# Edge rows of M as 32x32 TensorE tiles, four chunks at once, and M made by column halves

## The chip, the cores and the metric

The kernel runs on one core of one Trainium2 chip. The metric is device time in microseconds (us) of one execution. Besides the timed runs there is one profiled execution; its trace gives every duration below.

## What is computed

The reference is a sum of two blocks over the same 2048 x 640 activations `x`, in bf16:

```python
def reference(A_x, A_wqkv, A_wo, B_x, B_w_r, B_w_gate, B_w_up, B_w_down):
    def _A_ref(x, wqkv, wo):                      # linear attention, H = 32 heads of Dh = 20
        ...
        phi = lambda t: jnp.where(t > 0, t + 1, jnp.exp(t)) + 1e-6
        pq, pk = phi(q), phi(k)
        kv = jnp.einsum("bhsd,bhse->bhde", pk, v)
        z = jnp.einsum("bhsd->bhd", pk)
        num = jnp.einsum("bhqd,bhde->bhqe", pq, kv)
        den = jnp.einsum("bhqd,bhd->bhq", pq, z)[..., None] + 1e-6
        o = num / den
        return (lambda x, *d: x.transpose(*d))(o, 0, 2, 1, 3).reshape(B, S, D) @ wo
    def _B_ref(x, w_r, w_gate, w_up, w_down):     # 8 rows, chosen by x @ w_r, pass a gated MLP
        ...
        return x + upd.reshape(B, S, D)
    x = A_x
    xn = _layernorm(x, axis=-1)
    return x + _A_ref(xn, A_wqkv, A_wo) + _B_ref(xn, B_w_r, B_w_gate, B_w_up, B_w_down)
```

Since `num` is linear in `kv`, and `wo` follows it, the kernel makes one matrix M = blockdiag(kv) @ wo, of 640 x 640, and the output is the normalized phi(q) times M.

## The kernel before

The work is one program with its order written out by hand: each engine runs its instructions in the order of the code, and DMAs wait in the queue of the engine that issues them (SyncE, called SP, for nearly all).

**First part, up to about 52 us of the span.** For each of 16 token tiles of 128 rows: layer norm on VectorE and ScalarE, a transpose of xn (`tr_dma`, by DMA), the k projection on TensorE (`K`, L241), phi on ScalarE and VectorE, and the accumulation of G = xn^T phi(k) in PSUM (`G`, L281 and L286). `loads(t)`, called at the end of tile t, issues loads for later: at t = 13 wq, wo1 (the first 128 of each 160 rows of wo), wo2 (the last 32 of each 160 rows; chunk g lies on partitions 32g to 32g+31) and the gate weights.

**Middle part, to about 83 us.** phi(q) is made in 20 pieces: `q_pe(tb, m, bank)` (L489) is five matmuls of 512 columns, whose result ScalarE passes through Exp and Relu (L495, L496); `q_fin` (L544) joins the two on VectorE. Between these pieces stand kv, M, the denominators and the routed rows:

- `kv_pe` multiplies wv with G. Heads are 20 wide, and a chunk g of 160 columns holds eight of them; its block diagonal is cut into four row blocks of 32 (L633), which fill the 128 rows of `kv1`, and an edge of 32 rows (L640), which goes to `kv2`. `kv_ev` masks both on VectorE: four instructions for kv1 (L649) and four for the edges (L654), which put chunk g's edge on partitions 32g to 32g+31 and in columns 160g+120 to 160g+159 of `kv2`. Everything else of kv2 is zero.
- M has five row chunks of 128 rows (m = 0 to 4). In each, rows 32g to 32g+31 come from kv chunk g, by a slice of kv's columns with step 5 that starts at m (`by5`). `m_tiled(m, b)` (L659) makes them from kv1 as four 128x32 tiles side by side, for both column halves, into banks b and b+1. `m_full(m, b, eng)` (L665) adds the edges of all four kv chunks with one 128x128 matmul per half and evicts the chunk (L672 on VectorE, L670 on ScalarE) to `Mb`.
- `route1` and `route2` find the eight rows; `route2` ends with eight copies on GpSimd (L614) that gather xn's columns into `xsT`, each behind a register load. `gu_pe` (L683) is the gate and up projection, `y_pe` (L705) the down projection.
- `den` (L553) makes the denominators, `norm` (L579) multiplies phi(q) by their inverse.

The order around the change is: `kv_pe`, `kv_ev`, q_pe(0,4), q_fin(0,3), q_pe(1,0), q_fin(0,4), `route2`, q_pe(1,1), then m_tiled(0), m_tiled(1), m_full(0), m_full(1); three q pieces later the same for m = 2 and 3; four q pieces later m_tiled(4), and behind `den` and `gu_pe` m_full(4).

**Last part.** For each token tile ten matmuls with Mb (`out_mm`, L721), an addition on VectorE (L735) and a store.

Of the kernel before, what the change touches and what calls it, by code (L numbers as in the profile page):

```python
# [7 lines left out]
P = 128  # L8
S = 2048
D = 640  # L10
# [5 lines left out]
NG = 4  # L16
GC = D // NG
# [5 lines left out]
FQ = F // 4  # L23
# [6 lines left out]
BF16 = mybir.dt.bfloat16  # L30
F32 = mybir.dt.float32
I32 = mybir.dt.int32
I16 = mybir.dt.int16
AF = mybir.ActivationFunctionType
ALU = mybir.AluOpType
# [3 lines left out]
def kernel(  # L39
# [13 lines left out]
    pe, dve, act, pool, sp = nc.tensor, nc.vector, nc.scalar, nc.gpsimd, nc.sync  # L53
# [11 lines left out]
    PS = psp.tile([P, 8, 512], F32, name="PS")  # L65

    def st(shape, dt, name, tag=None):
        return sb.tile(shape, dt, name=name, tag=tag or name)
# [5 lines left out]
    wk = st([P, KC * (D + 1)], BF16, "wk", "wkM")  # L74
    wq = st([P, KC, D], BF16, "wq")
    wo1 = st([P, NG, D], BF16, "wo1")
    wo2 = st([P, D], BF16, "wo2")
    wv = st([P, KC, D], BF16, "wv")
    Gs = st([P, KC, D], BF16, "Gs")
    wg = st([P, KC, F], BF16, "wg")  # L80
# [5 lines left out]
    bm2 = st([P, GC], BF16, "bm2")  # L86
# [10 lines left out]
    HW = 320  # L97
# [4 lines left out]
    def ld(eng, dst, src):  # L102
        eng.dma_start(dst, src)
# [20 lines left out]
    def warm(n, w=512):  # L124
# [6 lines left out]
        out=ident[:], in_=ident[:], compare_op=ALU.not_equal, fill=1.0,  # L131
# [9 lines left out]
    kv1 = st([P, NG, GC], BF16, "kv1")  # L141
    kv2 = st([P, NG, GC], BF16, "kv2")
# [195 lines left out]
    wo_v = A_wo.rearrange("(g r) d -> r g d", r=GC)  # L338
    wg_v = B_w_gate.rearrange("(kc p) n -> p kc n", p=P)
    wu_v = B_w_up.rearrange("(kc p) n -> p kc n", p=P)  # L340

    def loads(t):
        if t < 5:
            ld(sp, XX[:, 6 + 2 * t : 8 + 2 * t, 1, :], x_v[:, 6 + 2 * t : 8 + 2 * t, :])
        if 7 <= t < 7 + KC:
            ld(sp, wv[:, t - 7, :], wqkv_v[:, t - 7, 2 * D : 3 * D])
        if t == 6:
            late["wvb"] = st([P, D], BF16, "wvb", "junk")
            ld(sp, late["wvb"][:], A_wqkv[ZD : ZD + 1, 2 * D : 3 * D].to_broadcast([P, D]))
        if t == 13:  # L350
            ld(sp, wq[:], wqkv_v[:, :, 0:D])
            ld(sp, wo1[:], wo_v[0:P, :, :])
            for g in range(NG):
                ld(sp, wo2[32 * g : 32 * g + 32, :], A_wo[GC * g + P : GC * (g + 1), :])
            for k in range(KC):
                ld(sp, wg[:, k, :], wg_v[:, k, :])


    ld(sp, XX[:, 4:6, 1, :], x_v[:, 4:6, :])
    loads(0)  # L360
    for t in range(1, 5):
        loads(t)
# [78 lines left out]
    for t in range(4, T):  # L441
# [36 lines left out]
        if t > 4:  # L478
            loads(t)


    def by5(ap):
        return ap.rearrange("p (q m) -> p m q", m=KC)
# [3 lines left out]
    def q_pe(tb, m, bank):  # L487
        for kc in range(KC):
            pe.matmul(  # L489
                PS[:, bank, :], lhsT=by5(wq[:, kc, :])[:, m, :], rhs=xnT[:, kc, tb * TBLK : (tb + 1) * TBLK],  # L490
                start=(kc == 0), stop=(kc == KC - 1),
            )
        e = tmp.tile([P, D], BF16, tag="ek", name="qe", bufs=3)[:, 0:TBLK]
        r = tmp.tile([P, D], BF16, tag="rk", name="qr", bufs=3)[:, 0:TBLK]
        act.activation(e, PS[:, bank, :], AF.Exp)  # L495
        act.activation(r, PS[:, bank, :], AF.Relu)  # L496
        qst[(tb, m)] = (e, r)
# [41 lines left out]
    Mb = st([P, KC, D + 1], BF16, "Mb", "wkM")  # L539
    rd_d = drp.tile([2, H, 8 * P], BF16, name="rd_d")  # L540

    def q_fin(tb, m):
        e, r = qst[(tb, m)]
        dve.scalar_tensor_tensor(  # L544
            out=pqT[:, m, tb * TBLK : (tb + 1) * TBLK], in0=e, scalar=1.0, in1=r,
            op0=ALU.min, op1=ALU.add,
        )

    def den(u, bank):
        for m in range(KC):  # L550
            for j in range(4):
                o = (4 * u + j) * 2 * P
                pe.matmul(  # L553
                    PS[32 * j : 32 * j + 32, bank, 0 : 2 * P], lhsT=zm[:, m, :], rhs=pqT[:, m, o : o + 2 * P],
                    start=(m == 0), stop=(m == KC - 1), skip_group_check=True,
                )

    def den_ev(u, bank):
        ld_ = tmp.tile([P, 2 * P], F32, tag="lden", name="lden")
        rd = tmp.tile([P, 2 * P], BF16, tag="rden", name="rden")  # L560
        act.activation(ld_[:], PS[:, bank, 0 : 2 * P], AF.Ln, bias=eps6[:])
        act.activation(rd[:], ld_[:], AF.Exp, scale=-1.0)
        ld(sp, rd_d[u, :, :].rearrange("h (j c) -> j h c", j=4), rd[:])
# [52 lines left out]
    def gates():  # L616
        act.activation(ge[:], r8[:].bitcast(F32), AF.Exp, scale=-1.0)
        act.activation(gl[:], ge[:], AF.Ln, bias=1.0)
        act.activation(g8[:], gl[:], AF.Exp, scale=-1.0)
        dve.tensor_copy(rowsf[:, 1, :, 0:C], g8[:].unsqueeze(1).to_broadcast([1, 4, C]))  # L620

    def route3():
        for k in range(2):
            ld(sp, cols[:, k : k + 1], rowsf[0:1, k, :, :].rearrange("o a b -> o (a b)"))

    KW = ((0, 40), (20, 80), (60, 100), (80, 140), (120, GC))

    def kv_pe(bank):
        for g in range(NG):
            for a in range(KC):  # L630
                for b in range(4):
                    w0, w1 = KW[b]
                    pe.matmul(PS[32 * b : 32 * b + 32, bank, g * 64 : g * 64 + w1 - w0],  # L633
                              lhsT=wv[:, a, g * GC + 32 * b : g * GC + 32 * b + 32],
                              rhs=Gs[:, a, g * GC + w0 : g * GC + w1],
                              start=(a == 0), stop=(a == KC - 1), skip_group_check=True)
        w0, w1 = KW[4]
        for a in range(KC):
# [5 lines left out]
    def kv_ev(bank):  # L644
        for b in range(4):
            w0, w1 = KW[b]
            r = slice(32 * b, 32 * b + 32)
            src = PS[r, bank, 0:256].rearrange("p (g c) -> p g c", c=64)[:, :, 0 : w1 - w0]
            dve.tensor_tensor(out=kv1[r, :, w0:w1], in0=src,  # L649
                              in1=bm1[r, w0:w1].unsqueeze(1).to_broadcast([32, NG, w1 - w0]), op=ALU.mult)  # L650
        w0, w1 = KW[4]
        for g in range(NG):
            r = slice(32 * g, 32 * g + 32)
            dve.tensor_tensor(out=kv2[r, g, w0:w1], in0=PS[r, bank, 256 : 256 + w1 - w0], in1=bm2[r, w0:w1], op=ALU.mult)  # L654

    def m_tiled(m, b):
        for h in range(2):
            for g in range(NG):
                pe.matmul(PS[32 * g : 32 * g + 32, b + h, 0:HW], lhsT=by5(kv1[:, g, :])[:, m, :],  # L659
                          rhs=wo1[:, g, h * HW : (h + 1) * HW],  # L660
                          start=True, stop=False, skip_group_check=True)

    def m_full(m, b, eng):
        for h in range(2):
            pe.matmul(PS[:, b + h, 0:HW], lhsT=by5(kv2[:].rearrange("p g c -> p (g c)"))[:, m, :],  # L665
                      rhs=wo2[:, h * HW : (h + 1) * HW],
                      start=False, stop=True, skip_group_check=True)
        dst = Mb[:, m, 0:D].rearrange("p (h c) -> p h c", h=2)
        if eng is act:
            act.copy(dst, PS[:, b : b + 2, 0:HW])  # L670
        else:
            eng.tensor_copy(dst, PS[:, b : b + 2, 0:HW])  # L672

    hf = [st([P, FQ], F32, "he"), st([P, FQ], F32, "hl")]
    hs = st([P, FQ], BF16, "hs")
    hh = st([P, FQ], BF16, "hh")
    hT = st([P, 3, P], BF16, "hT")
# [1 line left out]
    def gu_pe(b):  # L679
        for i, w in enumerate((wg, wu)):  # L680
            for kc in range(KC):
                for j in range(4):
                    pe.matmul(PS[32 * j : 32 * j + 32, b + i, P:512], lhsT=xsT[:, kc, :],  # L683
                              rhs=w[:, kc, j * FQ : (j + 1) * FQ],
                              start=(kc == 0), stop=(kc == KC - 1), skip_group_check=True)

    def gu_act(b):
        act.activation(hf[0][:], PS[:, b, P:512], AF.Exp, scale=-1.0)
        act.activation(hf[1][:], hf[0][:], AF.Ln, bias=1.0)
        act.activation(hs[:], hf[1][:], AF.Exp, scale=-1.0)  # L690

    def gu_ev(b):
        dve.tensor_tensor(out=hh[:], in0=PS[:, b, P:512], in1=hs[:], op=ALU.mult)
# [93 lines left out]
    q_fin(0, 2)  # L787
    kv_pe(3)
    kv_ev(3)
    q_pe(0, 4, 0)  # L790
    wd = st([P, F // P, D], BF16, "wd", "pkwd")
# [3 lines left out]
    q_fin(0, 4)  # L795
    route2()
    q_pe(1, 1, 2)
    m_tiled(0, 6)
    m_tiled(1, 4)
    m_full(0, 6, dve)  # L800
    m_full(1, 4, act)
    q_fin(1, 0)
    q_pe(1, 2, 0)
    q_fin(1, 1)
    q_pe(1, 3, 1)
    z_mask()
    q_fin(1, 2)
    m_tiled(2, 6)
    m_tiled(3, 4)
    m_full(2, 6, dve)  # L810
    m_full(3, 4, act)
    gates()
    route3()
    q_pe(1, 4, 2)
# [2 lines left out]
    q_fin(1, 4)  # L817
    q_pe(2, 1, 1)
    q_fin(2, 0)
    m_tiled(4, 4)  # L820
    den(0, 3)
    gu_pe(6)
    m_full(4, 4, dve)
    den_ev(0, 3)
    gu_act(6)
    bcast(0)
    hi_copy()
# [91 lines left out]
```

## Time and profile before

| | us |
|---|---|
| median of three runs (110.24 to 110.72) | 110.72 |
| the profiled execution, whole | 111.19 |
| its span, which the trace covers | 109.4 |
| TensorE busy with matmuls | 103.0 |
| VectorE busy | 85.9 |
| ScalarE busy | 74.7 |
| GpSimd busy | 21.8 |

The engines are PE (TensorE; PEld is its weight load), DVE (VectorE), ACT (ScalarE), POOL (GpSimd) and SP (SyncE). A line like L665 is a line of the kernel. A row of the timeline gives the start in us, the busy time, the engine, line and operation, what it writes and reads, the shape and the count, and in brackets how long the engine stood idle before it and what released it. A row of the chain gives start, length and the line. Matmuls are pipelined: the record of one is longer than the distance to the next.

### The profile page before, as it was taken

How to read it: one execution, taken by the hardware profiler on the slowest of the kernel's cores; microseconds unless marked ns; L12 is line 12 of the kernel's file. 1: busy time of each engine (PE TensorE's matmuls, PEld its weight loads, DVE VectorE, ACT ScalarE, POOL GpSimd, SP SyncE). 2: the span in 40 equal slices, each digit the busy share in tenths (PEclk: the TensorE clock that was granted, in tenths of full speed). 3: DMA queues.
4: the chain of work that ended last, by engine and by line, in shares of the span. 5: the costliest groups of instructions: out<-in, count | busy, mean ns of one | idle time of the engine just before them, and what ended most of it. 6: DMA issues, size and time to landing. Idle time of an engine off the chain costs nothing.

```text
span 109.4 us, 2507 instructions
## 1 busy us (share of the span) xinstructions
PE 103.0 (94%) x881; PEld 63.9 (58%) x891; DVE 85.9 (79%) x213; ACT 74.7 (68%) x163; POOL 21.8 (20%) x64
## 2 busy tenths in 40 slices
PE   5997999999999899999999999999999999999970
PEld 1355665665666466666556555565656677777740
DVE  1799988979999999874798997619778696788870
ACT  4628997877987778888497978997869499200000
POOL 7327113437322222000000013300006000000140
PEclk9999999999999999999999999999999999999999
DMA  2999930323576475379994999801370223895342
GB/s 76 272 304 364 283 70 16 63 59 63 124 152 136 99 155 113 64 211 382 353 367 114 325 346 382 286 22 42 121 261 6 61 88 128 184 358 211 128 140 92
DMA packets 22687, 19.19 MB, mean 175 GB/s; under 512 B 10514, under 2 KB 21138, under 8 KB 22674
## 3 DMA queue, kind: packets, MB, share of 16 engines
q1 hardware_dynamic: 22152, 18.92, 58.7%
q8 instruction: 7, 0.11, 0.4%
q10 hardware_dynamic: 234, 0.09, 0.3%
q0 software_dynamic: 288, 0.01, 0.3%
q14 instruction: 6, 0.05, 0.1%
HBM read 13.31 MB, written 3.65 MB: 155 GB/s over the span
## 4 chain that ended last, share of the span: by engine, by line
PE 62%; DVE 17%; DMA 7%; POOL 4%; ACT 4%; issue 2%; SPq 1%; DVEq 0%; ACTq 0%
PE PS L721 20%; PE PS L489 20%; PE PS L241 6%; PE PS L281 6%; DVE XX L203 4%; DMA xnT<-XX 4%; POOL s L189 4%; DVE pk L276 3%; DMA XX<-in_A_x_dram 3%; DVE stats L159 3%; DVE stats L156 2%; DVE MVf L162 2%; PE PS L659 2%; PE PS L665 2%; DVE t L187 1%
## 5 line engine op out<-in xcount | busy, mean ns | idle before, releaser
L241 PE MATMUL PS<-wk,xnT 128*128 128x320 bf16 (+1 forms) x160 | 24.6, 300 | 1.2 <-DMA wk<-in_A_wqkv_dram 0.6
L489 PE MATMUL PS<-xnT,wq 128*128 128x512 bf16 x95 | 22.6, 380 | 0.3
L281 PE MATMUL PS<-pk,XX 128*128 128x512 bf16 x75 | 22.4, 379 | 0.1
L721 PE MATMUL PS<-Mb,pqT 128*128 128x320 bf16 x160 | 22.1, 299 | 0.0
L241 PEld LDWEIGHTS <-xnT 128*128 128x128 bf16 x160 | 15.3, 98 | 8.5 <-DMA xnT<-XX 0.8
L721 PEld LDWEIGHTS <-pqT 128*128 128x128 bf16 x160 | 15.5, 97 | 6.5 <-issue 0.2
L257 ACT ACTIVATE ek<-PS 128x320 bf16<-128x320 f32 x32 | 14.2, 443 | 5.3 <-PE PS L241 5.3
L489 PEld LDWEIGHTS <-wq 128*128 128x128 bf16 x100 | 11.4, 118 | 8.6
L495 ACT ACTIVATE qe<-PS 128x512 bf16<-128x512 f32 x20 | 12.2, 609 | 4.8 <-PE PS L489 4.8
L544 DVE SCALAR_TENSOR_TENSOR pqT<-qe,qr 128x512 bf16<-128x512 bf16 x20 | 13.4, 684 | 2.2 <-ACT qr L496 2.1
L189 POOL TENSOR_TENSOR s<-t,halfc 128x1 bf16<-128x1 bf16 x16 | 9.9, 616 | 26.4 <-DVE t L187 26.4
L735 DVE TENSOR_TENSOR o<-PS,XX 128x640 bf16<-128x640 f32 x15 | 12.2, 821 | 3.5 <-PE PS L721 2.7
L260 ACT ACTIVATE rk<-PS 128x320 bf16<-128x320 f32 x32 | 14.3, 447 | 0.0
L286 PE MATMUL PS<-pk,XX 128*128 128x128 bf16 x64 | 14.0, 219 | 0.3
L276 DVE SCALAR_TENSOR_TENSOR pk<-ek,rk 128x640 bf16<-128x640 bf16 x16 | 13.0, 815 | 1.1 <-ACT rk L260 1.0
L281 PEld LDWEIGHTS <-XX 128*128 128x128 bf16 x80 | 7.7, 97 | 8.1
L496 ACT ACTIVATE qr<-PS 128x512 bf16<-128x512 f32 x20 | 12.1, 607 | 0.0
L194 ACT ACTIVATE c<-XX,MVf 128x640 bf16<-128x640 bf16 x10 | 8.4, 836 | 2.7 <-DVE MVf L162 1.9
L231 ACT ACTIVATE XX<-XX,MR,SR 128x640 bf16<-128x640 bf16 x11 | 9.4, 915 | 0.0
L156 DVE BATCH_NORM_STATS2 stats<-XX 128x6 f32<-128x320 bf16 x14 | 6.8, 486 | 2.0 <-DMA XX<-in_A_x_dram 1.9
L203 DVE TENSOR_SCALAR XX<-c,SR 128x640 bf16<-128x640 bf16 (+2 forms) x17 | 6.5, 389 | 1.7 <-ACT ek L257 0.5
L579 DVE TENSOR_TENSOR pqT<-pqT,R 128x1280 bf16<-128x1280 bf16 x8 | 6.5, 817 | 0.6 <-DMA R<-rd_d 0.6
(119 smaller groups left out, 102.4 us busy)
## 6 DMA issues: line engine op xcount, KB each, us to landing
out_dram<-o SPq DMA_DIRECT2D x15, 160.0 KB, 2.0
XX<-in_A_x_dram SPq DMA_DIRECT2D x6, 320.0 KB, 7.0
wg<-in_B_w_gate_dram SPq DMA_DIRECT2D x5, 384.0 KB, 5.7
wu<-in_B_w_up_dram SPq DMA_DIRECT2D x5, 384.0 KB, 5.9
wd<-in_B_w_down_dram SPq DMA_DIRECT2D x1, 1920.0 KB, 11.7
wk<-in_A_wqkv_dram SPq DMA_DIRECT2D x2, 400.0 KB, 4.8
wv<-in_A_wqkv_dram SPq DMA_DIRECT2D x5, 160.0 KB, 2.5
wq<-in_A_wqkv_dram SPq DMA_DIRECT2D x1, 800.0 KB
```

Source lines behind the costliest of these rows:

```text
L189: pool.tensor_tensor(out=ss[t][:], in0=t2[:], in1=halfc[:], op=ALU.pow)
L241: pe.matmul(PS[:, b + h, off(t, h) : off(t, h) + w], lhsT=xnT[:, kc, t * P : (t + 1) * P], rhs=wkh[h][:, kc, 0:w], start=(kc == 0), stop=( ...
L257: act.activation(phis[t][0][:, h * HW : (h + 1) * HW], phi_src(t, h, b), AF.Exp)
L260: act.activation(phis[t][1][:, h * HW : (h + 1) * HW], phi_src(t, h, b), AF.Relu)
L276: dve.scalar_tensor_tensor(out=pk[:, t, :], in0=ek[:], scalar=1.0, in1=rk[:], op0=ALU.min, op1=ALU.add)
L281: pe.matmul(PS[:, a, :], lhsT=lhsT, rhs=pk[:, t, 0:512], start=(t == 0), stop=(t == T - 1),)
L286: pe.matmul(PS[:, 5, a * P : (a + 1) * P], lhsT=lhsT, rhs=pk[:, t, 512:D], start=(t == 0 and a == 0), stop=(t == T - 1), skip_group_check= ...
L489: pe.matmul(PS[:, bank, :], lhsT=by5(wq[:, kc, :])[:, m, :], rhs=xnT[:, kc, tb * TBLK : (tb + 1) * TBLK], start=(kc == 0), stop=(kc == KC ...
L495: act.activation(e, PS[:, bank, :], AF.Exp)
L544: dve.scalar_tensor_tensor(out=pqT[:, m, tb * TBLK : (tb + 1) * TBLK], in0=e, scalar=1.0, in1=r, op0=ALU.min, op1=ALU.add,)
L721: pe.matmul(PS[:, b + h, 0:HW], lhsT=pqT[:, kc, t * P : (t + 1) * P], rhs=Mb[:, kc, h * HW : (h + 1) * HW], start=(kc == 0), stop=(kc == K ...
L735: dve.tensor_tensor(out=ot[:].rearrange("p (h c) -> p h c", h=2), in0=PS[:, b : b + 2, 0:HW], in1=XX[:, t, 1, :].rearrange("p (h c) -> p h ...
```

## The change

The edges of M are no longer added by a 128x128 matmul that reads mostly zeros. VectorE writes the four masked edges in one instruction to a new tile `kve` (chunk g on partitions 32g to 32g+31, 40 columns). GpSimd then copies each of them to all four groups of 32 partitions of `kv2`, 16 copies of 32x40. wo2 grows alike: each group of 32 partitions holds the edge rows of all four chunks; two of its four loads move to tile 12, ahead of wq, the others stay behind wo1.

With that, `m_edge(m, h, b, r)` is four 32x32 tiles: row group r of the array, column group g for kv chunk g. `m_half(h)` makes the column half h of the chunks m = 0 to 3 together: 16 tiled matmuls into banks 4 to 7, then 16 edge matmuls in which chunk m uses row group m, then two evictions of two banks each, on VectorE and ScalarE. The fifth chunk is done by both halves: m_tiled as before, and `m_last` with eight edge matmuls on row groups 0 and 1 and one eviction. The two float buffers of the gate (`hf`) move into the space of wv.

```diff
-    wo2 = st([P, D], BF16, "wo2")
+    wo2 = st([P, NG, D], BF16, "wo2")
...
+    def wo2_rows(rs):
+        for r in rs:
+            ld(sp, wo2[32 * r : 32 * r + 32, :, :], wo_v[P:GC, :, :])
...
+        if t == 12:
+            wo2_rows((0, 1))
         if t == 13:
             ld(sp, wq[:], wqkv_v[:, :, 0:D])
             ld(sp, wo1[:], wo_v[0:P, :, :])
-            for g in range(NG):
-                ld(sp, wo2[32 * g : 32 * g + 32, :], A_wo[GC * g + P : GC * (g + 1), :])
+            wo2_rows((2, 3))
...
         w0, w1 = KW[4]
+        dve.tensor_tensor(out=kve[:], in0=PS[:, bank, 256 : 256 + w1 - w0], in1=bm2[:, w0:w1], op=ALU.mult)
+        for r in range(4):
+            for g in range(NG):
+                pool.tensor_copy(kv2[32 * r : 32 * r + 32, g, w0:w1], kve[32 * g : 32 * g + 32, :])
+
+    def m_tiled(m, h, b):
         for g in range(NG):
-            r = slice(32 * g, 32 * g + 32)
-            dve.tensor_tensor(out=kv2[r, g, w0:w1], in0=PS[r, bank, 256 : 256 + w1 - w0], in1=bm2[r, w0:w1], op=ALU.mult)
-
-    def m_tiled(m, b):
+            pe.matmul(PS[32 * g : 32 * g + 32, b, 0:HW], lhsT=by5(kv1[:, g, :])[:, m, :],
+                      rhs=wo1[:, g, h * HW : (h + 1) * HW],
+                      start=True, stop=False, skip_group_check=True)
+
+    def m_edge(m, h, b, r):
+        for g in range(NG):
+            pe.matmul(PS[32 * g : 32 * g + 32, b, 0:HW], lhsT=by5(kv2[32 * r : 32 * r + 32, g, :])[:, m, :],
+                      rhs=wo2[32 * r : 32 * r + 32, g, h * HW : (h + 1) * HW],
+                      start=False, stop=True, skip_group_check=True)
+
+    def m_half(h):
+        for m in range(4):
+            m_tiled(m, h, 4 + m)
+        for m in range(4):
+            m_edge(m, h, 4 + m, m)
+        cs_ = slice(h * HW, (h + 1) * HW)
+        dve.tensor_copy(Mb[:, 0:2, cs_], PS[:, 4:6, 0:HW])
+        act.copy(Mb[:, 2:4, cs_], PS[:, 6:8, 0:HW])
+
+    def m_last():
         for h in range(2):
-            for g in range(NG):
-                pe.matmul(PS[32 * g : 32 * g + 32, b + h, 0:HW], lhsT=by5(kv1[:, g, :])[:, m, :],
...
-    def m_full(m, b, eng):
-        for h in range(2):
-            pe.matmul(PS[:, b + h, 0:HW], lhsT=by5(kv2[:].rearrange("p g c -> p (g c)"))[:, m, :],
-                      rhs=wo2[:, h * HW : (h + 1) * HW],
-                      start=False, stop=True, skip_group_check=True)
...
+            m_edge(4, h, 4 + h, h)
+        dve.tensor_copy(Mb[:, 4, 0:D].rearrange("p (h c) -> p h c", h=2), PS[:, 4:6, 0:HW])
...
     q_pe(1, 1, 2)
-    m_tiled(0, 6)
-    m_tiled(1, 4)
-    m_full(0, 6, dve)
-    m_full(1, 4, act)
+    m_half(0)
...
     q_fin(1, 2)
-    m_tiled(2, 6)
-    m_tiled(3, 4)
-    m_full(2, 6, dve)
-    m_full(3, 4, act)
+    m_half(1)
...
-    m_tiled(4, 4)
+    m_tiled(4, 0, 4)
+    m_tiled(4, 1, 5)
     den(0, 3)
     gu_pe(6)
-    m_full(4, 4, dve)
+    m_last()
```

More of the change, by code (lines that the diff above doesn't have):

```diff
@@ L624, in route3 @@
             ld(sp, cols[:, k : k + 1], rowsf[0:1, k, :, :].rearrange("o a b -> o (a b)"))
+    kve = st([P, 40], BF16, "kve")
     KW = ((0, 40), (20, 80), (60, 100), (80, 140), (120, GC))
@@ L651, in kv_ev @@
         w0, w1 = KW[4]
-        for g in range(NG):
-            r = slice(32 * g, 32 * g + 32)
-            dve.tensor_tensor(out=kv2[r, g, w0:w1], in0=PS[r, bank, 256 : 256 + w1 - w0], in1=bm2[r, w0:w1], op=ALU.mult)
-    def m_tiled(m, b):
-        for h in range(2):
-            for g in range(NG):
-                pe.matmul(PS[32 * g : 32 * g + 32, b + h, 0:HW], lhsT=by5(kv1[:, g, :])[:, m, :],
-                          rhs=wo1[:, g, h * HW : (h + 1) * HW],
-                          start=True, stop=False, skip_group_check=True)
@@ L663, in m_full @@
-    def m_full(m, b, eng):
-        for h in range(2):
-            pe.matmul(PS[:, b + h, 0:HW], lhsT=by5(kv2[:].rearrange("p g c -> p (g c)"))[:, m, :],
-                      rhs=wo2[:, h * HW : (h + 1) * HW],
-                      start=False, stop=True, skip_group_check=True)
[L668 to L674, printed above, removed]
+        dve.tensor_tensor(out=kve[:], in0=PS[:, bank, 256 : 256 + w1 - w0], in1=bm2[:, w0:w1], op=ALU.mult)
@@ new lines, in m_half @@
+    def m_half(h):
[7 more added lines that the diff above has]
+    def m_last():
+        for h in range(2):
+            m_edge(4, h, 4 + h, h)
+        dve.tensor_copy(Mb[:, 4, 0:D].rearrange("p (h c) -> p h c", h=2), PS[:, 4:6, 0:HW])
+    hb = st([P, 2, FQ], F32, "hb", "wv")
@@ L675 @@
+    hf = [hb[:, 0, :], hb[:, 1, :]]
     hs = st([P, FQ], BF16, "hs")
@@ L687, in gu_act @@
     def gu_act(b):
-        act.activation(hf[0][:], PS[:, b, P:512], AF.Exp, scale=-1.0)
-        act.activation(hf[1][:], hf[0][:], AF.Ln, bias=1.0)
-        act.activation(hs[:], hf[1][:], AF.Exp, scale=-1.0)
+        act.activation(hf[0], PS[:, b, P:512], AF.Exp, scale=-1.0)
+        act.activation(hf[1], hf[0], AF.Ln, bias=1.0)
+        act.activation(hs[:], hf[1], AF.Exp, scale=-1.0)
     def gu_ev(b):
```

## Prediction

> **What bounds the kernel now.** I read the chain of work that ended last first, the page's shares of it and then its pieces in order of time, because it says whose delay is the kernel's delay at the place of the change.
>
> ```profile
> PE 62%; DVE 17%; DMA 7%; POOL 4%; ACT 4%; issue 2%; SPq 1%; DVEq 0%; ACTq 0%
> ```
>
> ```profile
> 38.04 1.54 PE PS L241 x10
> ...
> 59.51 2.97 PE PS L489 x13
> 62.48 0.68 PE PS L659 x16
> 63.15 0.67 PE PS L665 x4
> 63.82 2.16 PE PS L489 x10
> 65.98 0.68 PE PS L659 x16
> 66.66 0.67 PE PS L665 x4
> ...
> 73.15 0.40 PE PS L665 x2
> ...
> 86.21 19.87 PE PS L721 x145
> 106.10 0.49 DVE o L731
> ```
>
> From 38.04 us to 106.10 us the chain is on TensorE alone, without a wait for another engine. The whole change lies inside this stretch. So whatever TensorE saves there is saved by the kernel, and whatever it waits there is lost in full: nothing behind 63 us has slack to give it back. The M chunks stand in the chain with L659 (the tiled part) and L665 (the edge part that goes): 0.67 + 0.67 + 0.40 us of L665 is all that the change can remove.
>
> **Step 1, TensorE.** Next the timeline around the first M block and the last, and two rows for how fast narrow matmuls follow each other.
>
> ```profile
> 62.41 0.75 PE L659 MATMUL PS<-wo,kv 128*32 128x320 bf16 x16
> 63.09 0.74 PE L665 MATMUL PS<-wo,kv 128*128 128x320 bf16 x4
> 63.66 2.32 PE L489 MATMUL PS<-xnT,wq 128*128 128x512 bf16 x10
> ...
> 73.08 0.47 PE L665 MATMUL PS<-wo,kv 128*128 128x320 bf16 x2
> 73.39 3.40 PE L489 MATMUL PS<-xnT,wq 128*128 128x512 bf16 x14
> ```
>
> ```profile
> L659 PE MATMUL PS<-wo,kv x40: 299/299/334, 62.4 to 70.7; 128*32 128x320 bf16 x40
> ```
>
> ```profile
> 58.14 0.70 PEld L633 LDWEIGHTS <-wv 128*32 128x32 bf16 x80 [0.41 <-issue]
> ...
> 78.05 0.81 PEld L705 LDWEIGHTS <-hT 128*32 128x32 bf16 x48 [0.40 <-issue]
> ```
>
> One L659 matmul is 0.30 us (the median of its line's own view), so the last of the 16 starts at 62.41 + 0.75 - 0.30 = 62.86, 30 ns behind its neighbour, and L665 follows at 63.09: 0.23 us from the last start of one tile shape to the first start of the next. From L665 to the next q projection (the same shape) there is no such gap: 63.53 to 63.66 is the pitch of L665 itself. So the old edge part costs 63.66 - 63.09 = 0.57 us.
>
> The new one issues 16 matmuls of 32x32 per half. No row shows that shape. The densest narrow stream, L633, has a pitch of about 7.7 ns (0.70 us less one load of about 0.1, over 79), L705, reckoned alike, one of 15 ns (160 columns wide), L659 one of 30 ns (320 columns, where the four column groups are busy). If the four row groups work side by side, the 16 tiles are all different and only issue counts: I take 7.7 ns, 15 x 7.7 = 0.12 us. If they work one after another it is the 30 ns of L659, 0.45 us. Behind it comes a change of shape that before did not have: 0.23 us. So 0.35 us in place of 0.57 us, 0.22 us won per half; at the other end 0.68 us, 0.11 us lost. The last chunk now costs 73.39 - 73.08 = 0.31 us; eight edge matmuls are 7 x 7.7 ns + 0.23 = 0.28 us, nothing won, or at 30 ns 0.44, 0.13 lost. If nothing else happened: 2 x 0.22 + 0.03, about 0.45 us won; at the other end 0.35 us lost. The evictions stay as they are, three of VectorE and two of ScalarE, 640 columns each; I cost them at nothing.
>
> The Trainium skill, "TensorE: Matmul & The Clock Gate", section "Measured speedup vs the span model", has 16 tiles of 32x32 running together with about 4 ns from one to the next; by it the edge part would be 15 x 4 ns + 0.23 = 0.29 us, and 0.06 us more would be won per half. No row here shows it, and the sum keeps 7.7 ns.
>
> **Step 2, the copies, which decide.** VectorE now writes the four edges in one instruction, and GpSimd spreads them in 16 copies of 32x40. TensorE needs all 16 before the last four edge matmuls of the first half. When can they start, and what does one take?
>
> ```profile
> 59.20 1.49 DVE L649 TENSOR_TENSOR kv<-PS,bm 32x160 bf16<-32x160 f32 x4
> 60.71 0.86 DVE L654 TENSOR_TENSOR kv<-PS,bm 32x40 bf16<-32x40 f32 x4
> 61.60 1.29 DVE L544 SCALAR_TENSOR_TENSOR pqT<-qe,qr 128x512 bf16<-128x512 bf16 x2
> ```
>
> ```profile
> 6.33 0.07 issue
> ```
>
> ```profile
> 60.85 0.59 ACT L496 ACTIVATE qr<-PS 128x512 bf16<-128x512 f32 x1
> ```
>
> The first L654 ends about 0.20 us (a quarter of 0.86) behind 60.71, at 60.91; a copy can start at 60.98 (the 0.07 us of issue that the chain has at 6.33 between VectorE's result and GpSimd's start). But VectorE is then free 0.66 us earlier (three of four L654, pitch 0.22 us), and the two q_fin (L544) move up to 60.93: their inputs are there, the second's last one at 60.85 + 0.59 = 61.44. They hold VectorE from 60.93 to 62.2, exactly where the copies want to run. What that does to them shows at the gather of route2, the only GpSimd copies that fall beside L544:
>
> ```profile
> 66.06 0.69 DVE L544 SCALAR_TENSOR_TENSOR pqT<-qe,qr 128x512 bf16<-128x512 bf16 x1
> 67.10 0.83 DVE L672 CAST Mb<-PS 128x640 bf16<-128x640 f32 x1 [0.35 <-PE PS L665]
> ...
> 69.62 0.69 DVE L544 SCALAR_TENSOR_TENSOR pqT<-qe,qr 128x512 bf16<-128x512 bf16 x1 [0.19 <-ACT qr L496]
> ```
>
> ```profile
> 64.94 0.34 POOL L614 COPY xsT<-xnT 128x5 bf16 x1 [17.56 <-DVE Mb L672]
> ...
> 66.38 0.44 POOL L614 COPY xsT<-xnT 128x5 bf16 x1 [0.50 <-issue]
> ...
> 67.77 0.20 POOL L614 COPY xsT<-xnT 128x5 bf16 x1 [0.49 <-issue]
> ...
> 69.85 0.53 POOL L614 COPY xsT<-xnT 128x5 bf16 x1 [0.34 <-issue]
> ```
>
> The copy of 66.38 takes 0.44 us and ends at 66.82, 0.07 us behind the L544 that ran to 66.75; that of 69.85 takes 0.53 us and ends at 70.38, 0.07 us behind the one that ran to 70.31. The copy of 67.77, begun beside the eviction of 67.10 to 67.93, keeps its 0.20 us. So a copy that meets an L544 waits for its end. In the trace, then, one copy slips in between the two q_fin and 15 remain from about 62.25 on.
>
> The Trainium skill, "SBUF — State Buffer", section "Who interferes with whom", states this as a lock: a VectorE instruction with two SBUF inputs and a GpSimd instruction that reads SBUF shut each other out for a whole instruction, and one with at most one such input does not. The trace agrees (0.07 us behind the end of L544, twice; nothing beside the eviction from PSUM).
>
> The price of a copy is unknown; the nearest rows:
>
> ```profile
> 0.31 0.10 POOL L903 MEMSET const-float32-0.0<- 128x1 f32 x1 [0.31 <-issue]
> 0.34 0.10 POOL L903 MEMSET const-float32-1.0<- 128x1 f32 x1
> ...
> 2.05 0.62 POOL L148 MEMSET kv<- 128x640 bf16 x1
> 2.63 0.22 POOL L149 MEMSET xsT<- 128x160 bf16 x1
> 2.81 0.28 POOL L150 CAST identf<-ident 128x128 f32<-128x128 bf16 x1
> ```
>
> An instruction that reads takes 0.20 us for 5 elements (L614) and 0.28 for 128 (L150), so about 0.225 us for 40. Neighbours overlap by 0.04 to 0.05 us (0.62 long, next start 0.58 later; 0.22 and 0.18), so one copy follows another by about 0.175 us. Lower end: tiny memsets follow by 0.03 us, and 480 more elements cost 0.40 us, so 0.03 + 0.03 = 0.06 us. Upper end: the whole 0.28 us of L150 with no overlap. I take 0.175, since L614 and L150 read SBUF as these do; that input and output lie on other partitions is unseen and may add to it.
>
> Last copy: 62.25 + 15 x 0.175 = 64.9 us. TensorE then needs 0.05 us of signal, four edge matmuls and the change of shape: the q projection starts at 64.9 + 0.05 + 0.02 + 0.23 = 65.2, not at 63.66: 1.54 us lost. The second half wins 0.22, the last chunk 0.03.
>
> **The rest, at nothing, and why.** GpSimd's gather stands behind the copies in its queue, and the gate and up matmuls (L683) wait for it.
>
> ```profile
> 71.24 1.52 PEld L683 LDWEIGHTS <-xsT 128*32 128x32 bf16 x40
> ```
>
> The last gather copy ends at 70.38 (above), 0.86 us ahead of that; copies that end at 64.9 push the gather about 1.0 us later (its first copy stands at 64.94 and one register load, up to 1 us, comes first), while TensorE comes 1.3 us later itself. It is hidden; without that shift it would cost about 0.2 us. The wo2 load grows from 160 to 640 KB (each of its four loads brings all four chunks' edges), and its first half moves ahead of wq, to SyncE's queue right before the last transpose of xn:
>
> ```profile
> GB/s 76 272 304 364 283 70 16 63 59 63 124 152 136 99 155 113 64 211 382 353 367 114 325 346 382 286 22 42 121 261 6 61 88 128 184 358 211 128 140 92
> ```
>
> ```profile
> 47.28 0.10 POOL L292 MEMSET XX<- 128x1 bf16 x1 [2.64 <-DMA xnT<-XX]
> ...
> 48.53 1.41 PEld L241 LDWEIGHTS <-xnT 128*128 128x128 bf16 x10
> ```
>
> That transpose has landed at 47.28 and is first read at 48.53: 1.25 us cover it. 320 KB more at the 353 to 382 GB/s of the slices from 49 to 57 us (each is 2.7 us long) are under 1 us, so nothing, or at worst a few tenths. What is pushed back behind it finds room in the slice of 57 to 60 us, where only 114 GB/s flow. The buffer shared with wv brings no wait: its last reader is L633 at 59 us, its first writer the gate at 72 us.
>
> **The sum.** 1.54 - 0.22 - 0.03 = +1.3 us. The profiled execution is 111.19 us with a span of 109.4, so about 112.5 and 110.7 after it; the median of the runs shown is 110.72, so **112.0 us**, 1.2% slower. A measurement of this kernel tells about 0.5% (0.55 us) from no change.
>
> **Rivals.** (a) **Not slower: the copies are hidden.** The place is the first edge matmul at 63.09; it decides if the last copy ends before it. That takes a pitch under 0.06 us behind the q_fin, or under 0.13 us (2.1 us for 16) with no waiting for them. For it: GpSimd's overlap of tiny instructions (0.03 us). Against it: the 0.20 us of every copy that reads. Then 0.45 us is won: 110.3 us, or 110.0 if the change of shape is cheaper than 0.23. (b) **The copies go ahead of the q_fin** (GpSimd asks first at 60.98 and keeps its turn, VectorE waits): last copy at 60.98 + 16 x 0.175 = 63.8, 0.4 us lost in the first half, net +0.2: 110.9. Against it: L614 waited each time. (c) **The row groups don't work at once**, so the edge part does not do what it says: in the first half the wait hides it but for the last four; the second half loses 0.11 in place of winning 0.22, the last chunk 0.13: with the wait +1.8, 112.5 us. (d) **Dear copies**, 0.28 us each: last one at 66.45, +2.9, 113.6 us.
>
> **How the numbers follow.** Forecast 0.52; (a) 0.20, half of it faster by over 0.5%; (b) 0.10, three quarters within 0.5%; (c) 0.10; (d) 0.08. Faster 0.10; same 0.10 + 0.07 + 0.02 (of the forecast, cheap copies) = 0.19; slower 0.71. The range takes in the forecast with a pitch of 0.12 to 0.25 us, (b), (c) and the nearer half of (a): 110.3 to 113.4.
>
> **What would show it.** The 16 copies in the timeline: their pitch, and whether they stand beside L544 at 61 to 62.2 us. TensorE idle before the first edge matmuls, with GpSimd as releaser, 1 to 2 us; none in the second half, where the q projection should start about 0.35 us behind the first edge matmul. GpSimd's gather ending before the gate matmuls. The forecast is wrong if the copies are done by 63 us, or if TensorE's lost time comes back before the last output.

## The result and the profile after

The changed kernel takes 114.16 us in the median (four runs, 113.68 to 115.94), against 110.72 us before: ratio 1.031, 95% interval 1.0275 to 1.0346. The forecast was slower, 112.0 us, range 110.3 to 113.4. The direction was right, the size was not. The profiled execution is the one of 115.94 us (span 114.2 us); its granted clock fell for some microseconds, and this ratio leaves it out.

The chain of work that ended last, from the place of the change on:

```profile
62.56 0.68 PE PS L665 x16
63.24 1.07 PE PS L671 x8
64.34 0.66 DVE Mb L681
...
65.05 0.21 POOL kv L661
...
65.94 0.57 POOL kv L661
...
66.56 0.60 PE PS L671 x2
67.16 1.12 PE PS L494 x4
...
68.50 2.34 PE PS L494 x5
70.84 0.90 PE PS L665 x14
71.74 0.30 PE PS L671 x16
```

Before, this stretch was TensorE alone. Now the chain leaves it: to the eviction on VectorE (L681), to the copies on GpSimd (L661), and back. L665 are now the tiled matmuls, L671 the edge matmuls, L494 the q projections. The first half's edge part lasts from 63.24 to 67.16, the second half's 0.30 us.

The timeline of the same stretch, rows of VectorE, GpSimd and TensorE:

```profile
60.80 0.20 DVE L658 TENSOR_TENSOR kve<-PS,bm 128x40 bf16<-128x40 f32 x1
60.92 1.33 DVE L549 SCALAR_TENSOR_TENSOR pqT<-qe,qr 128x512 bf16<-128x512 bf16 x2
61.06 5.71 POOL L661 COPY kv<-kve 32x40 bf16<-32x40 bf16 x16 [13.56 <-DVE kve L658]
...
64.34 0.83 DVE L681 CAST Mb<-PS 128x640 bf16<-128x640 f32 x1 [1.18 <-PE PS L671]
65.08 1.35 DVE L549 SCALAR_TENSOR_TENSOR pqT<-qe,qr 128x512 bf16<-128x512 bf16 x2
...
66.56 0.11 PEld L671 LDWEIGHTS <-kv 32*32 32x32 bf16 x1 [0.51 <-POOL kv L661]
66.83 0.11 PEld L671 LDWEIGHTS <-kv 32*32 32x32 bf16 x1 [0.16 <-POOL kv L661]
67.09 0.80 PEld L494 LDWEIGHTS <-wq 128*128 128x128 bf16 x5
```

The 16 copies start at 61.06, as forecast (60.98), but end at 66.77 and not at 64.9. TensorE takes the edges one by one as they come, and the q projection starts at 67.09; before it started at 63.66. TensorE lost 3.4 us there in place of the 1.54 of the forecast.

The clock of the profiled execution, 40 slices of 2.9 us:

```profile
PEclk9999999999999999999999985999999999999999
```

Soon behind the wait, at about 67.9, the clock falls to half until about 71.3: five q matmuls take 2.34 us (68.50), where five took about 1.08 before. That is a loss of its own, which the forecast did not have.

### The profile page after: what moved, and what is told of

The parts are those of the page before. It is cut to its first block, busy times and chain, and to the rows that moved or that the text cites. A ratio compares the mean times of both kernels' runs of the same rounds, so it can differ in the third digit from the quotient of the medians.

```text
span 114.2 us, 2581 instructions
## 1 busy us (share of the span) xinstructions
PE 106.8 (94%) x910; PEld 64.4 (56%) x921; DVE 85.2 (75%) x210; ACT 74.7 (65%) x163; POOL 26.0 (23%) x80
## 4 chain that ended last, share of the span: by engine, by line
PE 61%; DVE 17%; DMA 6%; POOL 5%; ACT 3%; issue 3%; SPq 1%; ACTq 0%; DVEq 0%; POOLq 0%
PE PS L494 20%; PE PS L737 19%; PE PS L241 6%; PE PS L281 5%; DVE XX L203 4%; POOL s L189 4%; DMA xnT<-XX 4%; DVE pk L276 3%; DMA XX<-in_A_x_dram 3%; DVE stats L159 3%; PE PS L671 2%; DVE stats L156 2%; PE PS L665 2%; DVE MVf L162 2%; DVE t L187 1%
## 5 line engine op out<-in xcount | busy, mean ns | idle before, releaser
L494 PE MATMUL PS<-xnT,wq 128*128 128x512 bf16 x94 | 24.1, 396 | 0.5 <-issue 0.2
L494 PEld LDWEIGHTS <-wq 128*128 128x128 bf16 x100 | 11.4, 120 | 9.7 <-issue 1.3
L661 POOL COPY kv<-kve 32x40 bf16<-32x40 bf16 x16 | 4.8, 303 | 14.4 <-DVE kve L658 13.6
```

What stands on the lines that cost most here:

```text
L494: pe.matmul(PS[:, bank, :], lhsT=by5(wq[:, kc, :])[:, m, :], rhs=xnT[:, kc, tb * TBLK : (tb + 1) * TBLK], start=(kc == 0), stop=(kc == KC ...
```

## The experiments

The theory after the result: TensorE loses the time by waiting for the copies; they are late because one follows the other by 0.27 us and not 0.175, and because q_fin on VectorE holds four of them, not two. Rivals: the 32x32 tiles, their change of shape, the halves or the larger load of wo2 cost the time; the price of a copy comes from something else than the number of copies. Each ratio below is against runs of the kernel before that were made together with it (medians 110.67 to 110.94 us).

**e1, evictions swapped.** ScalarE evicts chunks 0 and 1, VectorE 2 and 3.

```diff
-        dve.tensor_copy(Mb[:, 0:2, cs_], PS[:, 4:6, 0:HW])
-        act.copy(Mb[:, 2:4, cs_], PS[:, 6:8, 0:HW])
+        act.copy(Mb[:, 0:2, cs_], PS[:, 4:6, 0:HW])
+        dve.tensor_copy(Mb[:, 2:4, cs_], PS[:, 6:8, 0:HW])
```

> The changed kernel with the two evictions of each half swapped: ScalarE takes chunks 0 and 1, VectorE chunks 2 and 3. Theory (copies and their collisions): in the changed kernel VectorE evicted chunks 0 and 1 before the last copies were done, and two q_fin then ran beside the copies and held two of them for 0.35 us each. Now VectorE waits for the last edge matmul, so from the third copy on all follow at 0.27 us, the last ends 0.7 us sooner, and the kernel takes about 113.1 us in place of 113.8. Rival (a GpSimd copy is just slow, q_fin does not matter): 113.8. Rival (the tiles, their change of shape or the larger load cost the time): 113.8.

Measured: 113.89 us in the median (six runs, three of them with a dropped clock), ratio 1.0203 (1.0154 to 1.0251), in which one of these three still counts. The runs at full clock are 112.94, 113.14 and 113.34 us, against 113.68, 113.82, 113.84, 114.17 and 114.51 of the changed kernel: 0.7 us less, as expected. The copies in the timeline, first of e1, then the last ones of the changed kernel in a second trace (e8):

```profile
60.45 5.01 POOL L661 COPY kv<-kve 32x40 bf16<-32x40 bf16 x16 [13.22 <-DVE kve L658]
```

```profile
64.11 0.21 POOL L661 COPY kv<-kve 32x40 bf16<-32x40 bf16 x1
64.38 0.56 POOL L661 COPY kv<-kve 32x40 bf16<-32x40 bf16 x1
65.00 0.56 POOL L661 COPY kv<-kve 32x40 bf16<-32x40 bf16 x1
65.62 0.21 POOL L661 COPY kv<-kve 32x40 bf16<-32x40 bf16 x1
```

5.01 us in place of 5.71: the two copies of 0.56 us, which met the two q_fin, are gone. Undisturbed copies start every 0.27 us though each is 0.21 us long. That q_fin holds copies is shown; the rest of the loss is not explained by it.

**e2, edges made four times by TensorE, no copies.**

```diff
-        for a in range(KC):
-            for g in range(NG):
-                pe.matmul(PS[32 * g : 32 * g + 32, bank, 256 : 256 + w1 - w0],
+        for g in range(NG):
+            for a in range(KC):
+                for r in range(4):
+                    pe.matmul(PS[32 * r : 32 * r + 32, bank, 256 + 40 * g : 296 + 40 * g],
...
+        dve.tensor_tensor(out=kv2[:, :, w0:w1], in0=PS[:, bank, 256:416].rearrange("p (g c) -> p g c", g=NG),
+                          in1=bm2[:, w0:w1].unsqueeze(1).to_broadcast([P, NG, w1 - w0]), op=ALU.mult)
```

> The changed kernel without any GpSimd copy: kv_pe computes each chunk's edge four times, once per column group of the array (80 matmuls of 40 columns in place of 20), and one VectorE instruction masks all of them into kv2. Tiles, banks, halves and the load of wo2 stay as in the changed kernel. Theory: without the copies TensorE waits for nothing; 60 more narrow matmuls at 7.7 ns cost 0.46 us, the edge tiles win about 0.45: 110.7 us, between 110.3 and 111.2. Rival (tiles, change of shape, larger load): 112.5 us or more, as the copies were only covering it.

Measured: 110.61 us, ratio 0.9976 (0.9942 to 1.001): no difference from before that can be told. The chain of e2 (L647 are the 80 edge matmuls of kv_pe, L670 the edge tiles of M):

```profile
58.86 0.66 PE PS L647 x80
...
63.57 0.31 PE PS L670 x15
63.87 2.29 PE PS L494 x10
...
73.09 0.28 PE PS L670 x7
73.37 3.37 PE PS L494 x15
```

The edge tiles take 0.31 us where L665 took 0.67 before, and the ten q matmuls behind them 2.29 where they took 2.16: the change of shape. So 0.36 - 0.13 = 0.23 us is won per half, and nothing in the last chunk (0.28 and 0.13 more behind it, for 0.40). The 60 more matmuls cost 0.66 - 0.16 = 0.50 us, which takes it back. All that the rivals name is still in this kernel, the load of wo2 too; without the copies the 3.4 us are gone.

**e3, diagonal tiles, no copies.** Chunk g's edge stays on its own row group.

```diff
...
-            pe.matmul(PS[32 * g : 32 * g + 32, b, 0:HW], lhsT=by5(kv2[32 * r : 32 * r + 32, g, :])[:, m, :],
-                      rhs=wo2[32 * r : 32 * r + 32, g, h * HW : (h + 1) * HW],
+            pe.matmul(PS[32 * g : 32 * g + 32, b, 0:HW], lhsT=by5(kv2[32 * g : 32 * g + 32, 0, :])[:, m, :],
+                      rhs=wo2[32 * g : 32 * g + 32, g, h * HW : (h + 1) * HW],
```

> The changed kernel without copies in another way: chunk g's edge stays on partitions 32g and up, and its edge matmul is the diagonal tile of row group g and column group g for every m, so only four tiles work at once. Theory (wait for copies is the loss): no wait, and the 16 edge matmuls of a half take the 30 ns of the tiled ones; 0.11 us lost per half and 0.13 in the last chunk: 111.1 us. If the change of shape costs more than read, up to 111.5. Rival (load of wo2, halves, banks): 112.5 us or more.

Measured: 110.93 us, ratio 1.001 (0.9972 to 1.0048). Its chain:

```profile
62.89 0.67 PE PS L668 x16
63.56 2.29 PE PS L494 x10
```

With four tiles at once the edge part takes 0.67 us, as the full matmuls did, and the change of shape comes on top: 0.13 us lost per half (0.11 expected). Beside e2's 0.31 us this shows that the four row groups do work side by side. The 0.4 us of loss in all lies inside the interval.

**e4 and e12, the price of a copy by itself.** GpSimd instructions that nobody waits for, added to the kernel before behind hi_add.

```diff
     out_ev(0)
     hi_add()
+    for k in range(4):
+        pool.tensor_copy(wo1[32 * k : 32 * k + 32, 0, 40:80], kv1[32 * k : 32 * k + 32, 0, 40:80])
+    for k in range(4):
+        pool.tensor_copy(wo1[32 * k : 32 * k + 32, 1, 40:80], kv1[32 * (3 - k) : 32 * (3 - k) + 32, 1, 40:80])
...
```

> The kernel before, with 24 GpSimd instructions added behind hi_add, where nobody waits for them: four each of copies 128x40, copies 32x40 on their own partitions, copies 32x40 to other partitions, memsets 32x40, copies 128x1 and copies 128x160. The output is as before. Theory P1 (any GpSimd instruction that reads SBUF is over before the next begins): pitch 0.27 us for all three kinds of 40 elements, about 0.24 for 128x1, 0.36 for 128x160, and 0.06 for the memsets. Theory P2 (the shift to other partitions costs the gap): 0.17 us on own partitions, 0.27 only for the shifted ones. Time about 110.7 us.

> The kernel before, with 20 GpSimd copies of 40 columns behind hi_add, where nobody waits: five on partitions 0 to 31 alone, five of 64 partitions in turn on the lower and the upper half, five of 64 partitions on the lower half alone, five of 128. Theory A (a copy on part of the partitions does not overlap with the next): 0.25 us of pitch for the first three kinds, 0.15 to 0.17 for 128. Theory B (the change of partitions between neighbours costs the gap): 0.15 to 0.17 for the first and third kind, 0.25 for the second.

Measured: 111.2 and 110.97 us, one run each; nothing waits for the copies. From e4's timeline: copies to other partitions, memsets, and copies of 128 partitions.

```profile
86.89 0.21 POOL L861 COPY wo<-kv 32x40 bf16<-32x40 bf16 x1
87.14 0.21 POOL L861 COPY wo<-kv 32x40 bf16<-32x40 bf16 x1
...
88.57 0.12 POOL L863 MEMSET wo<- 32x40 bf16 x1
88.73 0.12 POOL L863 MEMSET wo<- 32x40 bf16 x1
...
90.52 0.32 POOL L867 COPY wo<-kv 128x160 bf16<-128x160 bf16 x1
90.78 0.32 POOL L867 COPY wo<-kv 128x160 bf16<-128x160 bf16 x1
```

32x40 copies follow every 0.25 us at 0.21 us of length, and those on their own partitions do the same (86.13, 86.38, 86.63): the shift costs nothing, so P2 is out. But 32x40 memsets, which read nothing, follow every 0.16 us at 0.12, and 128x160 copies, which read, every 0.26 at 0.32. So P1 is out too. What those with a gap share is that each stands on other partitions than the one before. e12 tests that:

```profile
87.03 0.21 POOL L860 COPY wo<-kv 64x40 bf16<-64x40 bf16 x1
87.28 0.22 POOL L860 COPY wo<-kv 64x40 bf16<-64x40 bf16 x1
...
88.78 0.37 POOL L862 COPY wo<-kv 64x40 bf16<-64x40 bf16 x2
89.09 0.21 POOL L864 COPY wo<-kv 128x40 bf16<-128x40 bf16 x1
89.25 0.81 POOL L864 COPY wo<-kv 128x40 bf16<-128x40 bf16 x1
```

64 partitions in turn on the lower and upper half (L860): every 0.25 us. The same 64 partitions each time (L862): two in 0.37 us, so the second begins 0.16 us after the first; 128 partitions (L864): 0.16 us. Theory B (the change of partitions costs the gap) holds for these kinds. The five copies on partitions 0 to 31 are 0.55 to 0.81 us long each, and most of that time no VectorE instruction with two SBUF inputs runs (the last ends at 85.20, the copies go on to 86.24). What held them is not shown, and no pitch is read from them. Nor is it shown why the pitch is 0.25 us in the probes and 0.27 in the changed kernel.

**e5, e6 and e7, M later.** The two halves stand behind q_pe(2,0) and q_pe(2,1), the fifth chunk and the gate matmuls behind q_pe(2,2).

```diff
     q_pe(1, 1, 2)
-    m_half(0)
     q_fin(1, 0)
...
     q_pe(2, 0, 0)
+    m_half(0)
     q_fin(1, 4)
     q_pe(2, 1, 1)
     q_fin(2, 0)
+    den(0, 3)
+    m_half(1)
...
```

> The changed kernel with the two halves of M moved behind the copies: m_half(0) after q_pe(2,0), m_half(1) after q_pe(2,1) and the denominators, the fifth chunk with the gate matmuls after q_pe(2,2); the gated MLP one q piece later throughout. The copies stay as they are and end at about 67 to 67.5 us, while m_half(0) comes at about 66.9. Theory: the copies are hidden but for 0.5 us at most, and TensorE's 0.45 us show: 110.3 us, between 110.0 and 111.0. Rival (copies cost by holding VectorE, or the tiles cost the time): 112 us or more.

> The kernel before in the same new order as e5: control for the order alone. Theory: M is needed only by the last part, so the order alone changes nothing: 110.7 us, within 0.4. If it is faster, e5's time has to be held against this one.

> e2 in the order of e5: edges made four times by TensorE, no copies, M later. Theory: as e2, 110.7 us within 0.4, since in neither case does TensorE wait for the edges; e5 should beat it by the 0.46 us of the 60 matmuls. Rival (the order hides something else): more than 0.5 us below e2.

Measured: e5 111.74 us, ratio 1.0062 (1.003 to 1.0094); e6 110.76, 0.9989 (0.9966 to 1.0011); e7 111.23, 1.0049 (1.0008 to 1.0091). The order alone costs nothing (e6). e5 takes back most of the loss, but not all: its chain, behind copies that took from 60.94 to 67.76, goes on over the gather:

```profile
67.55 0.21 POOL kv L661
...
72.83 0.20 POOL xsT L619
...
73.07 1.81 PE PS L699 x40
```

The gather stands behind the copies in GpSimd's queue, and now the gate matmuls (L699) wait for it until 73.07; in e6, the same order without copies, they (L683 there) begin at 72.17:

```profile
72.17 1.62 PE PS L683 x35
```

The wait had moved, not gone. The forecast for e5 had left this out. e7 is unexplained: against e6 its chain has 0.84 us less in the M blocks, 0.50 more in kv_pe and three times 0.13 behind the edges, +0.05 in all, and the medians differ by 0.47. That stays open. It was also expected to lose to e5 by 0.46 us, and did not, since e5 waits for the gather.

**e8, the changed kernel again.**

> The changed kernel again, for a trace at full clock. Expected 113.8 us; from the first copy's start to the last one's end 5.7 us as in the first trace, and TensorE's first q projection behind the first half 3.4 us later than before; no slice with the clock below 0.9.

Measured: 114.52 us, ratio 1.0289 (1.0236 to 1.0343). The copies start at 60.12 and take 5.71 us again. The expectation on the clock failed: two of four runs had it dropped, the profiled one (114.87 us, mean clock 0.985) and one of 120.06 us (0.957). The windows of the profiled one (the column behind the engines' busy times is the granted clock):

```profile
62.30:66.30 4.00, 3.41 (x17) 1.27 (x18) 2.34 (x4) 0.44 (x1) 3.15 (x12) 0.92 0.98 354
66.30:70.00 3.70, 3.70 (x15) 1.33 (x18) 0.25 (x1) 1.78 (x3) 1.03 (x5) 0.62 1.04 355
```

In the wait TensorE does 17 matmuls in 4 us; in the 3.7 us behind it the mean clock is 0.62. The drop begins shortly before the wait is over, whose mean is 0.92.

**e9, edges masked first.**

```diff
     def kv_ev(bank):
+        w0, w1 = KW[4]
+        dve.tensor_tensor(out=kve[:], ...)          # and the 16 copies
         for b in range(4):
...
```

> The changed kernel with VectorE masking the edges ahead of kv1 in kv_ev: all else, the 16 copies too, as it is. The copies then start at about 59.5 us, 1.5 us sooner, and five of them run beside the kv1 masks, which read PSUM and do not hold them up; two pass between the two q_fin, nine follow from 62.4 on at 0.27 us, and two more are held 0.35 us each by the q_fin behind the first eviction. Theory (pitch and collisions): the last one ends at 65.3 to 65.5 in place of 66.8, the kernel takes about 112.3 us, 1.5 below the changed one, and with a wait of 2 us in place of 3.4 the granted clock drops seldom or never. Rival (the clock drop is the change's and not the wait's): it drops as often as before.

Measured: 111.38 us, ratio 1.0063 (1.003 to 1.0096), and in none of ten runs a clock below 0.995. GpSimd's row, and the first half's edge part in the chain:

```profile
58.88 4.94 POOL L655 COPY kv<-kve 32x40 bf16<-32x40 bf16 x16 [11.45 <-DVE kve L652]
```

```profile
62.57 1.62 PE PS L671 x16
```

The first edge part is 1.62 us in place of 3.9, 1.3 more than without a wait; less the 0.23 won twice that is +0.85, and +0.7 was measured. It is 0.9 better than expected: the last copy began ahead of the q_fin at 63.66, so the second meeting that the expectation had priced at 0.7 us did not happen.

**e10 and e11, six copies in place of 16.** The edges go straight into slot 0 of kv2; four copies turn them by one row group, two of 64 partitions by two. e11 has them ahead of kv1 as in e9.

```diff
...
+        dve.tensor_tensor(out=kv2[:, 0, w0:w1], in0=PS[:, bank, 256 : 256 + w1 - w0], in1=bm2[:, w0:w1], op=ALU.mult)
+        for r in range(4):
+            s = (r - 1) % 4
+            pool.tensor_copy(kv2[32 * r : 32 * r + 32, 1, w0:w1], kv2[32 * s : 32 * s + 32, 0, w0:w1])
+        for r, s in ((64, 0), (0, 64)):
+            pool.tensor_copy(kv2[r : r + 64, 2:4, w0:w1], kv2[s : s + 64, 0:2, w0:w1])
...
-            pe.matmul(..., lhsT=by5(kv2[32 * r : 32 * r + 32, g, :])[:, m, :],
+            pe.matmul(..., lhsT=by5(kv2[32 * r : 32 * r + 32, (r - g) % 4, :])[:, m, :],
```

> The changed kernel with 6 copies in place of 16: the edges are written straight into slot 0 of kv2, four copies 32x40 turn them by one row group into slot 1, and two copies of 64 partitions and 2x40 columns turn slots 0 and 1 by two row groups into slots 2 and 3; the edge matmuls pick the slot (r - g) mod 4. Theory: two copies pass with the two q_fin, four follow by 63.6 us; TensorE waits 0.3 us in the first half and wins 0.23 in the second: 110.8 us, between 110.4 and 111.3. If the price of a copy goes with its size and not its number, 111.5 or more.

> e10 with the edges masked ahead of kv1, as in e9: the copies run from 59.5 to 61.3 us beside the kv1 masks and are over before the first edge matmul at 63.1. Theory: nothing of the copies is left, and what the tiles win on TensorE shows alone: 2 x 0.23 = 0.45 us below the kernel before, 110.3 us (ratio 0.996). Rival (the tiles win nothing): 110.7.

Measured: e10 110.58 us, ratio 0.9979 (0.9947 to 1.0011); e11 110.08 us, ratio 0.9946 (0.9911 to 0.9981), 0.5% below the kernel before. In e10 the six copies run from 60.57 to 62.52, and TensorE starts on the edges at about 62.2. The rest of the first half's edge part in its chain:

```profile
62.57 0.38 PE PS L673 x14
```

The q projection starts at 62.88, so this edge part lasts 0.66 us in place of 0.31: 0.35 us of waiting, where 0.3 was expected. The two copies of 64x80 follow each other by 0.29 us, not much more than the 0.25 of the 32x40 ones, with four times the elements. e11's copies, and the first half's edge part in its chain:

```profile
59.38 0.96 POOL L655 COPY kv<-kv 32x40 bf16<-32x40 bf16 x4 [12.06 <-DVE kv L652]
60.40 1.33 POOL L657 COPY kv<-kv 64x80 bf16<-64x80 bf16 x2
```

```profile
62.61 0.31 PE PS L673 x16
```

The four copies beside the kv1 masks keep their 0.25 us of pitch; the last two meet the q_fin and are over at 61.73, before the first edge matmul at 62.61. Nothing waits, and the edge part takes 0.31 us in the first half too, as in the second. The 0.45 us of the tiles would be a ratio of 0.996, well inside the interval.

## Why the prediction was wrong

The mechanism was right: TensorE waits for the copies, the wait is lost in full, VectorE's two-input instructions hold the copies up, and a rewrite that hides them leaves a small win (e11). Sizes failed, in step 2.

- **"One copy follows another by about 0.175 us"** is the step that failed. Measured: 0.267 us in the changed kernel. The length of a copy was about right (0.225 us forecast, 0.21 measured); the overlap with the next was not. The overlap of 0.05 us was read from neighbours that all stood on 128 partitions; copies on changing partitions leave a gap instead (e4, e12). The prediction's upper end of the pitch, 0.28 us, held the value, but its range went only to 0.25. Rival (d), with 0.28 us and a chance of 0.08, gave 113.6 us and came nearest; its pitch was a little too dear, and it too had no second meeting with q_fin, so that it came so near is in part luck. From the third copy (62.38) 14 x 0.267 give 66.1 for the end, where 62.25 + 15 x 0.175 gave 64.9: 1.2 us.
- **A second meeting with q_fin** was missed. The prediction asks when TensorE has all 16 edges, and says nothing of what VectorE does meanwhile. The eviction of chunks 0 and 1 needs only the first eight copies; behind it two q_fin ran beside the last copies and held two of them, 0.7 us (e1). Of the two q_fin that it did foresee, the price was about right: two copies are over when the third starts at 62.38, where one was expected to be over at 62.25.
- Together 1.9 us: 112.0 + 1.9 = 113.9, and the five runs of the changed kernel at full clock have a median of 113.84. The trace adds up too: 3.4 us lost in the first half less 0.2 won in the second are 3.2, and 113.84 - 110.72 = 3.1.
- **The clock** was not in the forecast. Where it drops, it adds 1 to 2 us, once 6: 114.87, 115.94 and 120.06 us beside 113.84; in e1 114.45, 115.08 and 115.15 beside 113.14.
- **Step 1 was right.** With 16 tiles at once 0.22 us per half were forecast to be won and 0.23 were (e2), and in the last chunk nothing, as forecast. With four tiles at once the forecast was 0.11 us lost per half and 0.13 in the last chunk; e3 lost 0.13 and 0.13. One part was off: the 16 matmuls of a half take 0.38 us in all and 0.326 each (e2), so they start about 4 ns apart and not 7.7. That won 0.06 us more than forecast, and the change of shape behind them took it back: 0.26 us to the first q matmul and 0.03 in the ten q matmuls, where 0.23 was forecast. That the two cancel is luck.
- **The load of wo2** cost nothing, as forecast: e2, e3 and e11 have it whole. **The gather** was hidden in the changed kernel, as forecast, since TensorE came later still; e5 shows what it costs when TensorE does not.

The Trainium skill, "SBUF — State Buffer", section "Who interferes with whom", was borne out for the instructions met here: two q_fin taken from beside the copies gave back their 0.7 us (e1), and beside the kv1 masks, with one SBUF input, the copies kept 0.21 us (e11). The section also names VectorE modes, the 2-port ones, that contend with GpSimd; the prediction left them out, and no run here tests them.

## What to carry to other kernels

A new instruction chain on an idle engine is priced by the distance between its instructions, taken from neighbours that change what these change, and not by their length; then one asks which other engine's instructions hold it up in that time, also behind each wait that ends early. Small copies are priced by their count more than by their bytes: six for 16, put ahead of the work that does not need them, turned 3% of loss into 0.5% of win. And when an engine is made to wait, one looks at what stands behind it in the other's queue: with M moved later, the wait passed on to the gather.

## What the runs showed of the hardware

GpSimd instructions on the same partitions overlap by some 0.05 us (copies of 40 columns every 0.16 us at 0.21), those on changing partitions leave 0.04 to 0.06 (32x40 copies every 0.25 to 0.27 at 0.21). Which of the two it is does not hang on size, reading or the shift to other partitions in the kinds tried (e4, e12).

The granted clock fell for some microseconds in 6 of the 14 runs of the changed kernel, e8 and e1, whose traces show a first edge part of 3.3 to 4.0 us. It fell in none of ten runs of e9, where that part lasts 1.6 us, and in no run of the kernel before, whose lowest mean clock is 0.994. In all three traces with a drop the clock is half for 3.41 us. In the changed kernel it is 0.89 in the half microsecond from 67.5, 0.50 from 68.0 to 71.0 and 0.70 in the next half microsecond: 0.11 + 3.0 + 0.30 us at half (a mean of 0.89 over 0.5 us is 0.11 us at half clock). In e8, from 65.68 on, it is 0.32 + 3.0 + 0.09, in e1, from 65.22 on, 0.28 + 3.0 + 0.13. In e8 and e1 the drop begins before the edge part is over (66.27 and 65.90). The run of 120.06 us has no trace; its mean clock of 0.957 over 118.3 us would be 10.2 us at half clock, three such stretches (an estimate).

The Trainium skill, "TensorE: Matmul & The Clock Gate", section "What's actually happening", has the clock halved after an idle window of about 3.4 us, in windows that run freely and are not reset when a kernel starts. The traces agree with the half clock; a drop that lasts as long as such a window, and drops in some executions and not in others, fit it. But TensorE was not idle in the 3.4 us ahead of the drops: it did 12 matmuls there in the changed kernel, 19 in e8 and 31 in e1. How much work still counts as idle, and that the window is the cause, was not tried.

16 matmuls of 32x32 on 16 different tiles run together: their piece of the chain is 0.31 us long (e2, e11), against 0.67 us when only four tiles differ (e3).
